# Splitting the first four chunks of an FFN that follows block-sparse attention: half of the units early, the rest behind later chunks

## The chip, the cores and the metric

The kernel runs on one core of a Trainium2 chip. The metric is the device time of one execution in microseconds (us), the median of several runs. The engines are PE (TensorE, matmuls), PEld (its weight loads), DVE (VectorE), ACT (ScalarE), POOL (GpSimd) and SP (SyncE, which here only issues DMAs).

## What is computed

Block-sparse attention over 4 batches, 8 heads, 768 rows and 64 columns per head, in blocks of 32 rows, and then a feed-forward network with a rational function in the middle. A row block sees its neighbours, the first and the last block and three sampled ones; the first and the last block see everything.

```python
mask = np.abs(blk_i - blk_j) <= 1
mask = mask | (blk_i == 0) | (blk_j == 0) | (blk_i == n_blocks - 1) | (blk_j == n_blocks - 1)
...                                                  # and three sampled key blocks per query block
scores = np.where(mask, scores, -1000000000.0)
attn = np.exp(scores - np.max(scores, axis=-1, keepdims=True))
attn = attn / (np.sum(attn, axis=-1, keepdims=True) + 1e-09)
x = (attn @ v)                                       # then heads side by side: 3072 tokens x 512
h = x @ w_in                                         # 512 x 2048
P = a[0] + a[1] * h + a[2] * h * h + a[3] * h * h * h
Q = 1.0 + np.abs(b[0]) * np.abs(h) + np.abs(b[1]) * h * h
out = (P / (Q + 1e-6)) @ w_out                       # 2048 x 512
```

q, k and v are float32; the weights of the FFN arrive as float64.

## The kernel before

**Tiling.** The 3072 tokens are 12 chunks of 256 (three per batch). The 2048 hidden columns are 8 units of 256. One unit of one chunk is 24 matmuls into `ph` (L1078 to L1080, split float16 x against split weights), the rational function on ACT and DVE (L1085 to L1123), and 12 matmuls into the single accumulator `acc` (L1135, L1137, L1141). When a chunk's eight units are through, ACT copies `acc` to a load slot `ld` and SP stores it.

**Attention** goes by pairs of row blocks. `block(j)` gives the row block of position j; a usual pair is one part, the pair of the first and the last block (at position `J`) is three. A part is scores (L834), masked maxima on DVE (L846), exp on ACT (L865), transposes of the probabilities on PE (L914), values (L960) and the division (L986); 14 parts make a batch, 56 all. Batch 0 reads its keys from SBUF ("near", through the tile `kx`); for later batches the turned keys are stored to DRAM (`ks`) and POOL gathers them for each part into a key buffer (L792 to L801): one buffer is the front part of `kall`, which holds batch 0's keys until its last near scores, two more are made when the weights are decoded. Values are gathered by SP (`vg`, L929 to L939). Every four blocks, x is turned and split into float16 halves in one of three buffers: for chunks below `XD` by PE (`turn_x`, L999), for later ones by transposing DMAs (L1025).

**Weights** are decoded from float64 on the chip, in 16 pieces of w_in (two units each take four) and 16 of w_out (two per unit): ACT, POOL or DVE converts, DVE packs the bits (L452, L455, L459) and makes the low parts (L525), POOL subtracts (L475). Each piece has a due place: the first place in `order` at which its unit is wanted.

**Order.** Every operation is an `Op` with an engine, a price, what it follows, and a due time `prio` counted in places of the list `order`. `issue` builds the instruction streams: of the operations that are due no more than 8 places ahead of the last unit issued, it takes the one that can start first by the prices, and by due time among those; the streams are then fixed. `Ring` and `Slot` stand for buffers. `order` lists (chunk, unit); the list index is the place. Before, chunk 0 runs units 0 to 3, chunk 1 all eight, chunk 0 units 4 to 7, and then chunk by chunk. The first half's sum of chunk 0 waits in two of the three load slots (`kept`). `part_prio` gives the due time of attention parts, `when` that of a batch's preparation. PE fills idle time with matmuls of no use (L162) until the first accumulator is in use.

Of the kernel before, what the change touches and what calls it, by code (L numbers as in the profile page):

```python
# [11 lines left out]
F32 = mybir.dt.float32  # L12
# [12 lines left out]
def kernel(  # L25
# [27 lines left out]
    nc = tc.nc  # L53
# [230 lines left out]
    r_ld, r_kt = Ring([p3] * 3), Ring([p1])  # L284
    r_ldq, r_qt, r_fc, r_ks = Ring([None]), Ring([None] * 2), Ring([None] * 2), Ring([None] * 2)
    r_xn, r_x16 = Ring([None]), Ring([])
# [56 lines left out]
    def scales(get, name, after, prio, slot=(), finish=None, keep=None):  # L343
# [9 lines left out]
        def largest():  # L353
            m = p4.tile([P, 12], F32, name=name, bufs=3)
            res.append(m)
            nc.vector.tensor_reduce(out=m[:, 0:1], in_=d["pt"][:, :P], axis=AX.X, op=ALU.max)
# [47 lines left out]
    HU = 4  # L404
    order = [(0, u) for u in range(HU)] + [(1, u) for u in range(NU)] + [(0, u) for u in range(HU, NU)] + [(c, u) for c in range(2, NC) for u in range(NU)]
    place = {cu: n for n, cu in enumerate(order)}

    def weights():
# [5 lines left out]
        for u in range(NG):  # L414
            pieces += [(min(place[0, 2 * u], place[1, 2 * u]) + -4.91, 0, u, x) for x in range(NCC)]
        for x in range(NF):
            pieces.append((min(place[0, x // 2], place[1, x // 2]) + x % 2 / 2 + 0.45, 1, x // NCC, x))
        pieces.sort(key=lambda p: p[0])
# [119 lines left out]

    J = (NT // 2 + 1) * TB - 2

# [22 lines left out]
    k_turned = {}  # L563
    ext = []

# [3 lines left out]
    def new_ld(slot):  # L569
        return slot.buf.tile([P, 512], F32, name="ld", bufs=3 if ext and slot.buf is ext[0] else None)  # L570

# [161 lines left out]
    ends = {}  # L733
    kxs = early.tile([P, 2, 2 * NR + 2, HG, BLK], F32, name="kx", bufs=1)

# [6 lines left out]
    def attention(b, j, prio):  # L742
# [296 lines left out]
    last_near = []  # L1039
    XB, XD = 4, 2  # L1040
    x_group = {}


    fcs, o_fc, accs, s_acc, kept = {}, {}, {}, {}, {}

    def factors(b, u, n, after, prio):

        def run():
            if b not in fcs:
                fcs[b] = p2.tile([P, 4, NU], F32, name="fc")  # L1050
# [10 lines left out]
    def unit(c, u):  # L1061

        b, k0 = c // NCH, place[c, u]
        new, last = u == 0 or (c == 0 and u == HU), u == NU - 1 or (c == 0 and u == HU - 1)
        d = {}
        s_ph, s_sq, s_tt, s_ab, s_rr, s_gh, s_gl = [Slot(r) for r in (r_ph, r_sq, r_tt, r_ab, r_rr, r_gh, r_gl)]

        def into(e):
            def run():
                xh, xl = xs_of[c]  # L1070
                d["cst"] = fcs[b][:, :, u]
# [70 lines left out]

        deps = (o_ready[c] + [o_fc[b, u]] if u == 0 else [o_fc[b, u]]) + (in_ready[u * CH // WC] if c < 2 else [])
        pk = [k0 + x for x in FO]
        i0 = Op(TE, 1307, into(0), deps, pk[0], behind=chain.get("into"), takes=[s_ph], uses=[s_xs[c]], unit=k0)
        i1 = chain["into"] = Op(TE, 1307, into(1), [i0], pk[1], uses=[s_ph, s_xs[c]])
        a = Op(SC, 571, square, [i1], pk[2], takes=[s_sq], uses=[s_ph])
# [11 lines left out]
        if new:  # L1159
            s_acc[c] = Slot(r_acc)  # L1160
        wo = out_ready[2 * u] + out_ready[2 * u + 1] if c < 2 else []
        o = Op(TE, 1690, out_high, [h] + wo, pk[11], behind=chain.get("out"), takes=[s_acc[c]] if new else [], uses=[s_gh] + ([] if new else [s_acc[c]]))
# [3 lines left out]
        for t in range(CH // P):  # L1166
            def store(t):
                if u == NU - 1 and (c, t) in kept:
                    s_ob, e, o1 = kept[c, t]
                else:  # L1170
                    s_ob, e, o1 = kept[c, t] = Slot(r_ld), {}, None
                acc = s_acc[c]

                def copy(eng):
# [11 lines left out]

                if o1:
                    a = Op(VE, 602, add, [o, o1], pk[12], uses=[s_ob, acc])
# [6 lines left out]
                if o1:  # L1195
                    s_ob.left -= 1
                Op(SY, [(475, 262144 // len(runs(c % NCH * 2 + t)))] * len(runs(c % NCH * 2 + t)), write, [a], pk[12], uses=[s_ob])
# [42 lines left out]
    for c, u in order:  # L1240
        b = c // NCH
        if b == 0 and u % (WC // CH) == 0 and (b, u) not in o_fc:
            factors(0, u, WC // CH, [scale_ready[u * CH // WC], v_scale[0], o_setup], place[c, u] - 1)
        elif b and (b, u) not in o_fc:
            factors(b, 0, NU, [scale_ready[g] for g in range(NG)] + [v_scale[b]], place[c, u] - 2)
        unit(c, u)

    def switch():
        early_cm.__exit__(None, None, None)
        ext.append(ctx.enter_context(tc.tile_pool(name="ext", bufs=1)))  # L1250
        t = max(o.end for o in decoded + last_near)
        r_ld.free += [(t, ext[0])] * 3
        r_x16.free.append((t, None))
        r_kt.free.append((t, kall[:, NP:NP + KB]))
        for j in range(2):
            kgs.append(ext[0].tile([P, NP, HG, BLK], F32, name=f"xkg{j}"))
            r_kg.free.append((t, len(kgs) - 1))

    Op(None, 0, switch, decoded + last_near, -1)
    ctx.enter_context(tc.manual_schedule(engines={getattr(mybir.EngineType, n) for n in (TE, SC, VE, PO, SY)}))  # L1260
# [30 lines left out]
```

## Time and profile before

| | us |
|---|---|
| median of 3 runs | 812.71 (812.38 to 813.65) |
| the profiled execution | 816.15 |
| its span, first to last instruction | 814.5 |
| PE busy | 769.2 |
| DVE busy | 667.9 |
| ACT busy | 570.8 |
| POOL busy | 228.0 |

A busy PE is pipelined matmuls whose ends are modelled, so it shows that PE is never waited for, not that it runs at its peak. PEclk is the granted share of TensorE's 2.4 GHz. L12 is line 12 of the kernel.

### The profile page before, as it was taken

What the parts mean: (1) busy time and instruction counts of PE and PEld (TensorE: products, weight loads), DVE (VectorE), ACT (ScalarE), POOL (GpSimd) and SP (SyncE); (2) the same over time, 40 slices, a digit from 0 to 9 for tenths busy, and PEclk for the clock granted to TensorE, in tenths of its full rate; (3) what the DMA queues carried; (4) which work ended last, traced back from release to release, by engine and by line L of the source; (5) the groups of instructions that cost most, each with busy time, mean ns of one, the idle gap of its engine ahead of it and who ended that gap; (6) DMA issues with size and microseconds to landing.
All of it is one profiled execution on the core that took longest, in us unless ns stands there. A gap on an engine that the chain in (4) does not pass through costs nothing.

```text
span 814.5 us, 26163 instructions
## 1 busy us (share of the span) xinstructions
PE 769.2 (94%) x10147; PEld 542.9 (67%) x10147; DVE 667.9 (82%) x1567; ACT 570.8 (70%) x1266; POOL 228.0 (28%) x401
## 2 busy tenths in 40 slices
PE   7898867799799998999999999999999999999997
PEld 4556645666577677677776667676776767767774
DVE  3878999999968995888887884887878876889986
ACT  2667875977767769768576769677676758767663
POOL 3506342334731025105332043205422044000000
PEclk9999988999899999999999999999999999999999
DMA  8987966446666866846665974857756746320000
GB/s 218 224 223 237 262 196 218 123 126 183 181 163 174 197 168 182 227 121 195 163 139 153 233 154 151 211 150 195 173 113 157 163 121 197 88 80 14 1 27 27
DMA packets 189916, 128.82 MB, mean 158 GB/s; under 512 B 84672, under 2 KB 170816, under 8 KB 189792
## 3 DMA queue, kind: packets, MB, share of 16 engines
q1 hardware_dynamic: 176640, 91.87, 44.0%
q0 software_dynamic: 13152, 35.28, 15.1%
q8 instruction: 81, 1.33, 0.7%
q14 instruction: 43, 0.35, 0.2%
HBM read 110.83 MB, written 11.01 MB: 150 GB/s over the span
## 4 chain that ended last, share of the span: by engine, by line
PE 79%; DVE 11%; ACT 3%; SPq 2%; issue 2%; DMA 2%; ACTq 0%; DVEq 0%
PE acc L1135 10%; PE ph L1078 10%; PE acc L1141 9%; PE acc L1137 9%; PE ph L1079 9%; PE ph L1080 9%; PE m L834 6%; PE av L960 6%; PE m L914 6%; PE acc L162 2%; PE m L560 2%; DVE tt L1092 1%; DMA ldq<-in_q_dram 1%; DVE pr L846 1%; DVE ab L1116 1%
## 5 line engine op out<-in xcount | busy, mean ns | idle before, releaser
L1078 PE MATMUL ph<-xh,wi 128*128 128x256 f16 x768 | 212.1, 276 | 11.3 <-DVE tt L1095 11.3
L1079 PE MATMUL ph<-xl,wi 128*128 128x256 f16 x768 | 211.7, 276 | 0.0
L1080 PE MATMUL ph<-xh,wi 128*128 128x256 f16 x768 | 211.4, 275 | 0.0
L1085 ACT ACTIVATE sq<-ph,fc 128x512 f32<-128x512 f32 x96 | 65.8, 685 | 104.7 <-PE ph L1080 104.2
L865 ACT ACTIVATE pr<-pr,st 128x256 f32<-128x256 f32 x224 | 110.9, 502 | 11.7 <-DVE st L877 11.5
L1135 PE MATMUL acc<-wo_h,gh 128*128 128x512 f32 x384 | 115.0, 422 | 1.4 <-ACT ld L150 0.7
L1141 PE MATMUL acc<-wo_b,gl 128*128 128x512 bf16 x384 | 99.6, 382 | 1.9 <-DVE gl L1123 1.9
L1137 PE MATMUL acc<-wo_l,gh 128*128 128x512 bf16 x384 | 100.1, 383 | 0.0
L1102 DVE SCALAR_TENSOR_TENSOR ab<-sq,absb,ab 128x512 f32<-128x512 f32 x96 | 73.3, 764 | 30.8 <-ACT ab L1099 30.7
L1113 DVE SCALAR_TENSOR_TENSOR gh<-tt,par,rr 128x512 fp32r<-128x512 f32 x96 | 72.9, 759 | 31.1 <-PE acc L1137 23.7
L1078 PEld LDWEIGHTS <-wi 128*128 128x128 f16 x768 | 76.3, 99 | 32.8 <-DVE tt L1095 9.6
L846 DVE CUSTOM_DVE_ANT_1 pr<-m,bias 128x256 f32<-128x256 f32 x204 | 76.4, 419 | 16.2 <-PE m L834 15.7
L1079 PEld LDWEIGHTS <-wi 128*128 128x128 f16 x768 | 75.9, 99 | 15.5 <-issue 2.9
L150 ACT ACTIVATE pT<-m 128x512 f32<-128x512 f32 x112 | 64.8, 594 | 29.5 <-PE m L914 27.7
L801 POOL DMA_DIRECT2D xkg<-ks x126 | 67.9, 539 | 52.1 <-issue 49.3
L1080 PEld LDWEIGHTS <-wi 128*128 128x128 f16 x768 | 76.0, 99 | 9.5
L914 PE MATMUL m<-ident,pr 128*128 128x128 f32 x448 | 71.5, 290 | 7.4 <-ACT pT L150 5.9
L1106 ACT ACTIVATE rr<-ab 128x512 f32<-128x512 f32 x96 | 60.4, 630 | 25.8 <-DVE ab L1102 23.6
L1092 DVE TENSOR_TENSOR tt<-tt,sq 128x512 f32<-128x512 f32 x96 | 70.7, 737 | 9.2 <-ACT tt L1089 9.0
L1135 PEld LDWEIGHTS acc<-wo_h,gh 128*128 128x128 f32 x384 | 66.5, 191 | 16.5 <-issue 2.2
L1089 ACT ACTIVATE tt<-ph,par,fc 128x512 f32<-128x512 f32 x96 | 75.1, 782 | 0.2
L914 PEld LDWEIGHTS m<-ident,pr 128*128 128x128 f32 x448 | 64.0, 206 | 15.0 <-ACT pT L150 6.3
(151 smaller groups left out, 1335.7 us busy)
## 6 DMA issues: line engine op xcount, KB each, us to landing
vg<-in_v_dram SPq DMA_DIRECT2D x312, 64.0 KB, 3.2
vg<-in_v_dram SPq DMA_DIRECT2D x88, 192.0 KB, 3.7
wl<-in_moe_w_out_dram SPq DMA_DIRECT2D x16, 512.0 KB, 4.3
xkg<-ks POOLq DMA_DIRECT2D x126, 64.0 KB, 3.1
vg<-in_v_dram SPq DMA_DIRECT2D x12, 512.0 KB, 4.5
xkg<-ks POOLq DMA_DIRECT2D x21, 256.0 KB, 3.6
ldq<-in_q_dram SPq DMA_DIRECT2D x20, 256.0 KB, 4.4
out_dram<-ld SPq DMA_DIRECT2D x20, 256.0 KB, 3.2
```

Source lines behind the costliest of these rows:

```text
L846: nc.vector.tensor_tensor_reduce(out=prs[x][:, e, g].rearrange("p (s r) -> p s r", r=BLK), in0=h["sp"][g][:, e], in1=add.rearrange("p (s o ...
L865: nc.scalar.activation(out=prs[x][:, e, g], in_=prs[x][:, e, g], func=AF.Exp, scale=SCALE, bias=st[:, 12 + y:13 + y], accum_out=st[:, 16 + ...
L914: nc.tensor.transpose(pp[:, jj * P:(jj + 1) * P], pr[:, e, g, kt:NS * BLK:2], ident)
L1078: nc.tensor.matmul(o, wh, xh[:, :, cc], start=(cc == 0), stop=False)
L1079: nc.tensor.matmul(o, wh, xl[:, :, cc], start=False, stop=False)
L1080: nc.tensor.matmul(o, wl, xh[:, :, cc], start=False, stop=(cc == NCC - 1))
L1089: nc.scalar.activation(out=d["tt"], in_=d["ph"], func=AF.Identity, scale=d["cst"][:, 3:4], bias=par[:, 2:3])
L1092: nc.vector.tensor_tensor(out=d["tt"], in0=d["tt"], in1=d["sq"], op=ALU.mult)
L1102: nc.vector.scalar_tensor_tensor(out=d["ab"], in0=d["sq"], scalar=absb[:, 1:2], in1=d["ab"], op0=ALU.mult, op1=ALU.add)
L1135: nc.tensor.matmul(acc, g, wo_h[:, f], start=(new and e == 0), stop=False)
L1137: nc.tensor.matmul(acc, g, wo_l[:, f], start=False, stop=False)
L1141: nc.tensor.matmul(acc, g, wo_b[:, f], start=False, stop=(last and e == 1))
```

## The change

Four chunks are split instead of one. Chunks 0 to 3 run units 0 to 3 at places 0 to 15, chunk 4 runs whole at places 16 to 23, and then each second half is followed by a whole later chunk: (0, 4 to 7), (5, all), (1, 4 to 7), (6, all), up to chunk 8; chunks 9 to 11 follow whole. The due places of the weights follow from that: units 4 to 7 are first wanted at places 20 to 23. The split x of chunks 0 to 3 is written to DRAM behind their first unit and read back ahead of unit 4; the partial sums go to DRAM too and are read back, and DVE adds them. The pair of the first and the last block moves to the last position of each batch (chunks 2, 5, 8, 11 instead of 1, 4, 7, 10). x is turned by PE for chunks below 6 instead of below 2. The `kx` tile is kept for the whole kernel and becomes a key buffer when the last near scores are done; behind the decoding come one more key buffer and two load slots instead of two and three. Due times of parts and preparation are moved to fit. The core of the diff:

```diff
-    order = [(0, u) for u in range(HU)] + [(1, u) for u in range(NU)] + [(0, u) for u in range(HU, NU)] + [(c, u) for c in range(2, NC) for u in range(NU)]
+    SPLIT = 4
+    order = [(c, u) for c in range(SPLIT) for u in range(HU)] + [(SPLIT, u) for u in range(NU)]
+    for c in range(SPLIT):
+        order += [(c, u) for u in range(HU, NU)] + [(SPLIT + 1 + c, u) for u in range(NU)]
+    order += [(c, u) for c in range(2 * SPLIT + 1, NC) for u in range(NU)]
     place = {cu: n for n, cu in enumerate(order)}
+    soonest = [min(place[c, u] for c in range(NC)) for u in range(NU)]
...
-            pieces += [(min(place[0, 2 * u], place[1, 2 * u]) + -4.91, 0, u, x) for x in range(NCC)]
+            pieces += [(soonest[2 * u] + -4.91, 0, u, x) for x in range(NCC)]
...
-    J = (NT // 2 + 1) * TB - 2
+    J = NB - 2
...
-    kxs = early.tile([P, 2, 2 * NR + 2, HG, BLK], F32, name="kx", bufs=1)
+    kxs = const.tile([P, 2, 2 * NR + 2, HG, BLK], F32, name="kx")
...
-                early_x = x < 5
+                early_x = x < 4
...
-    XB, XD = 4, 2
+    XB, XD = 4, 6
...
+        split = c < SPLIT
+        new, last = u == 0 or (split and u == HU), u == NU - 1 or (split and u == HU - 1)
+        xk = (c, 1) if split and u >= HU else c
...
+        if split and u == 0:
+            def put():
+                xd_of[c] = scr.tile([P, 2, CB * NCC * BLK], F16, name="xd", bufs=SPLIT)
+                for y in range(2):
+                    nc.sync.dma_start(out=xd_of[c][:, y], in_=xs_of[c][y].rearrange("p b c r -> p (b c r)"))
+
+            o_xd[c] = Op(SY, [(475, 262144)] * 2, put, o_ready[c], k0 + 1.2, uses=[s_xs[c]])
+        if split and u == HU:
+            s_xs[xk] = Slot(r_xs)
+
+            def get():
+                xs_of[xk] = xbufs[s_xs[xk].buf]
+                for y in range(2):
+                    nc.sync.dma_start(out=xs_of[xk][y].rearrange("p b c r -> p (b c r)"), in_=xd_of[c][:, y])
+
+            deps.append(Op(SY, [(475, 262144)] * 2, get, [o_xd[c]], k0 + 5.5, takes=[s_xs[xk]]))
...
+                if split and u == NU - 1:
+                    f = Op(SY, [(475, 262144)], fetch, [o_pd[c, t]], pk[12], takes=[s_ob])
+                    a = Op(VE, 602, add, [o, f], pk[12], uses=[s_ob, acc])
...
                 if u < NU - 1:
-                    s_ob.left += 1
-                    kept[c, t] = s_ob, e, a
+                    o_pd[c, t] = Op(SY, [(475, 262144)], put, [a], pk[12], uses=[s_ob])
                     return
...
-        if c == 2:
-            since = 9.1
         if c == 1:
             return by + (0.56 * (x + 1 - need[1])) - 1
+        if c <= SPLIT:
+            return since + (by - since) * (x + 1 - need[c - 1]) / (need[c] - need[c - 1]) - c
...
-        A = [8.9, 8.52] if b == 1 else [11.69, 8.81]
-        return lambda w, stage, j: p0 - A[stage] + (w * 6 + j) * (([0.5, 0.5] if b == 1 else [0.85, 0.83])[stage])
+        A = [6.5, 5.5] if b == 1 else [11.69, 8.81]
+        return lambda w, stage, j: p0 - A[stage] + (w * 6 + j) * (([0.45, 0.4] if b == 1 else [0.85, 0.83])[stage])
...
+    def switch_keys():
+        t = max(o.end for o in last_near)
+        kgs.append(kxs.rearrange("p y s h r -> p (y s) h r")[:, 0:NP])
+        r_kg.free.append((t, len(kgs) - 1))
+        r_kt.free.append((t, kall[:, NP:NP + KB]))
...
+        kgs.append(ext[0].tile([P, NP, HG, BLK], F32, name="xkg"))
+        r_kg.free.append((t, len(kgs) - 1))
+
+    Op(None, 0, switch_keys, last_near, -1)
+    Op(None, 0, switch, decoded, -1)
```

## Rows read from the trace of the kernel before

**Rows 1.** The page: busy us by engine; busy tenths in 40 slices of the span.

```profile
PE 769.2 (94%) x10147; PEld 542.9 (67%) x10147; DVE 667.9 (82%) x1567; ACT 570.8 (70%) x1266; POOL 228.0 (28%) x401
...
PE   7898867799799998999999999999999999999997
...
DVE  3878999999968995888887884887878876889986
```

**Rows 2.** Windows: stretch and length; PE, PEld, DVE, ACT, POOL busy us; clock, DMA share, GB/s.

```profile
62.00:222.00 160.00, 131.70 (x1875) 95.11 (x1875) 152.96 (x332) 121.89 (x273) 70.98 (x94) 0.91 0.65 191
222.00:304.00 82.00, 82.00 (x1107) 57.95 (x1100) 68.82 (x173) 55.60 (x127) 19.23 (x36) 1.00 0.71 177
304.00:740.00 436.00, 431.69 (x5683) 308.39 (x5682) 344.91 (x825) 317.44 (x714) 118.22 (x211) 1.00 0.62 158
...
755.00:800.00 45.00, 45.00 (x311) 32.04 (x308) 40.19 (x61) 29.33 (x48) 0.00 (x0) 1.00 0.04 13
```

**Rows 3.** Chain of waits, 755 to 800 us: start us, length us, what.

```profile
757.00 0.94 PE acc L1135 x4
...
799.40 0.94 PE acc L1135 x4
```

**Rows 4.** Windows of line L1078 alone: PE and PEld busy, instruction counts in brackets.

```profile
62.00:222.00 160.00, 35.02 (x120) 12.61 (x120) 0.91 0.65 191
222.00:304.00 82.00, 24.33 (x89) 8.77 (x90) 1.00 0.71 177
304.00:740.00 436.00, 126.66 (x464) 45.60 (x464) 1.00 0.62 158
```

**Rows 5.** Windows of line L865 alone: ACT busy, count; clock, DMA share, GB/s.

```profile
0.00:62.00 62.00, 8.80 (x35) 0.94 0.86 220
62.00:222.00 160.00, 22.73 (x87) 0.91 0.65 191
222.00:304.00 82.00, 12.51 (x48) 1.00 0.71 177
304.00:740.00 436.00, 72.74 (x280) 1.00 0.62 158
```

**Rows 6.** Chain of waits, 56 to 135 us.

```profile
121.36 3.03 DVE wi L525 x4
...
128.82 0.33 PE ph L1078
```

**Rows 7.** Waits of PE, 62 to 222 us: total us, times, longest us.

```profile
PE ph L1078 <- DVE tt L1095: 10.6, 5, 4.1
```

**Rows 8.** Chain of waits, 56 to 62 us: one group of transposes of x.

```profile
57.08 0.43 PE m L999 x4
```

**Rows 9.** Groups by line, DVE, whole span: busy us, mean ns, then idle before.

```profile
L1179 DVE TENSOR_TENSOR ld<-ld,acc 128x512 f32<-128x512 f32 x2 | 1.3, 684 | 0.9 <-PE acc L1141 0.9
```

**Rows 10.** The page, DMA issues: count, KB each, us to landing.

```profile
xkg<-ks POOLq DMA_DIRECT2D x126, 64.0 KB, 3.1
```

**Rows 11.** Timeline of PE around 184 and 199 us: start us, length us.

```profile
183.81 0.43 PE L834 MATMUL m<-kall,qt 64*32 64x96 f32 x15
...
198.56 1.10 PE L960 MATMUL av<-vg,pT 128*32 128x64 f32 x64
199.59 1.09 PE L834 MATMUL m<-kall,qt 64*32 64x256 f32 x32
```

**Rows 12.** Timeline of POOL, 190 to 260 us: one gather, first and last issue.

```profile
201.09 0.70 POOL L794 DMA_DIRECT2D kall<-ks  x1 [7.18 <-PE m L834]
...
205.31 0.54 POOL L801 DMA_DIRECT2D kall<-ks  x1 [0.16 <-issue]
```

**Rows 13.** Groups by line and form, DVE and POOL, 62 to 222 us.

```profile
L1092 DVE TENSOR_TENSOR tt<-tt,sq 128x512 f32<-128x512 f32 x15 | 15.1, 1008 | 0.4 <-ACT tt L1089 0.4
...
L475 POOL TENSOR_TENSOR wo_l<-dw,wo_h 128x512 bf16<-128x512 f32 x16 | 23.1, 1450 | 13.5 <-ACT wo_h L150 13.0
```

**Rows 14.** The same for DVE, 304 to 740 us.

```profile
L1092 DVE TENSOR_TENSOR tt<-tt,sq 128x512 f32<-128x512 f32 x58 | 39.8, 686 | 6.3 <-ACT tt L1089 6.1
```

More of the change, by code (lines that the diff above doesn't have):

```diff
@@ L353, in largest @@
         def largest():
-            m = p4.tile([P, 12], F32, name=name, bufs=3)
+            m = p4.tile([P, 12], F32, name=name, bufs=B)
             res.append(m)
@@ L414, in weights @@
         for u in range(NG):
-            pieces += [(min(place[0, 2 * u], place[1, 2 * u]) + -4.91, 0, u, x) for x in range(NCC)]
+            pieces += [(soonest[2 * u] + -4.91, 0, u, x) for x in range(NCC)]
         for x in range(NF):
-            pieces.append((min(place[0, x // 2], place[1, x // 2]) + x % 2 / 2 + 0.45, 1, x // NCC, x))
+            pieces.append((soonest[x // 2] + x % 2 / 2 + 0.45, 1, x // NCC, x))
         pieces.sort(key=lambda p: p[0])
@@ L563 @@
     k_turned = {}
-    ext = []
+    ext, EL = [], 2
     def new_pr():
@@ L569, in new_ld @@
     def new_ld(slot):
-        return slot.buf.tile([P, 512], F32, name="ld", bufs=3 if ext and slot.buf is ext[0] else None)
+        return slot.buf.tile([P, 512], F32, name="ld", bufs=EL if ext and slot.buf is ext[0] else None)
     def keys(b, t, prio, before, slot, new):
@@ L1049, in run @@
             if b not in fcs:
-                fcs[b] = p2.tile([P, 4, NU], F32, name="fc")
+                fcs[b] = p2.tile([P, 4, NU], F32, name="fc", bufs=B)
             nc.vector.scalar_tensor_tensor(out=fcs[b][:, :, u:u + n], in0=coefs.rearrange("p (j o) -> p j o", o=1).broadcast_to([P, 4, n]), scalar=v_inv[b],
@@ L1141, in out_low @@
                 nc.tensor.matmul(acc, g, wo_b[:, f], start=False, stop=(last and e == 1))
-        deps = (o_ready[c] + [o_fc[b, u]] if u == 0 else [o_fc[b, u]]) + (in_ready[u * CH // WC] if c < 2 else [])
+        deps = (o_ready[c] if u == 0 else []) + [o_fc[b, u]] + (in_ready[u * CH // WC] if c <= SPLIT else [])
         pk = [k0 + x for x in FO]
-        i0 = Op(TE, 1307, into(0), deps, pk[0], behind=chain.get("into"), takes=[s_ph], uses=[s_xs[c]], unit=k0)
-        i1 = chain["into"] = Op(TE, 1307, into(1), [i0], pk[1], uses=[s_ph, s_xs[c]])
+        if split and u == 0:
[11 more added lines that the diff above has]
+            deps.append(Op(SY, [(475, 262144)] * 2, get, [o_xd[c]], k0 + 5.5, takes=[s_xs[xk]]))
+        i0 = Op(TE, 1307, into(0), deps, pk[0], behind=chain.get("into"), takes=[s_ph], uses=[s_xs[xk]], unit=k0)
+        i1 = chain["into"] = Op(TE, 1307, into(1), [i0], pk[1], uses=[s_ph, s_xs[xk]])
         a = Op(SC, 571, square, [i1], pk[2], takes=[s_sq], uses=[s_ph])
@@ L1167, in store, with fetch, put @@
             def store(t):
[L1168 to L1171, printed above, removed]
+                s_ob, e = Slot(r_ld), {}
                 acc = s_acc[c]
+                def fetch():
+                    e["ob"] = new_ld(s_ob)
+                    nc.sync.dma_start(out=e["ob"], in_=pd_of[c][:, t])
+                def put():
+                    if c not in pd_of:
+                        pd_of[c] = scr.tile([P, CH // P, DM], F32, name="pd", bufs=SPLIT)
+                    nc.sync.dma_start(out=pd_of[c][:, t], in_=e["ob"])
                 def copy(eng):
@@ L1241 @@
         b = c // NCH
-        if b == 0 and u % (WC // CH) == 0 and (b, u) not in o_fc:
-            factors(0, u, WC // CH, [scale_ready[u * CH // WC], v_scale[0], o_setup], place[c, u] - 1)
-        elif b and (b, u) not in o_fc:
+        if b < 2 and u % (WC // CH) == 0 and (b, u) not in o_fc:
+            factors(b, u, WC // CH, [scale_ready[u * CH // WC], v_scale[b], o_setup], place[c, u] - 1)
+        elif b > 1 and (b, u) not in o_fc:
             factors(b, 0, NU, [scale_ready[g] for g in range(NG)] + [v_scale[b]], place[c, u] - 2)
         unit(c, u)
+    def switch_keys():
[3 more added lines that the diff above has]
+        r_kt.free.append((t, kall[:, NP:NP + KB]))
     def switch():
@@ L1250, in switch @@
         ext.append(ctx.enter_context(tc.tile_pool(name="ext", bufs=1)))
-        t = max(o.end for o in decoded + last_near)
-        r_ld.free += [(t, ext[0])] * 3
+        t = max(o.end for o in decoded)
+        r_ld.free += [(t, ext[0])] * EL
         r_x16.free.append((t, None))
[L1254 to L1259, printed above, removed]
+        kgs.append(ext[0].tile([P, NP, HG, BLK], F32, name="xkg"))
+        r_kg.free.append((t, len(kgs) - 1))
+    Op(None, 0, switch_keys, last_near, -1)
+    Op(None, 0, switch, decoded, -1)
     ctx.enter_context(tc.manual_schedule(engines={getattr(mybir.EngineType, n) for n in (TE, SC, VE, PO, SY)}))
```

13 lines of the change are left out of this document (4 added, 9 removed).

## The prediction

> **What bounds the kernel now.** The page comes first: PE is busy 94% of the span and DVE 82%, yet the slices say that these averages hide two stages: up to the eleventh slice DVE is the fuller engine, behind it PE is at 9 throughout [rows 1]. The windows give the border [rows 2]. From 62 us (first FFN unit) to 222 us DVE is busy 152.96 of 160 us and PE 131.70; from 222 to 304 PE is busy all 82 us and DVE 68.82; from 304 to 740 PE is busy 431.69 of 436 us. So behind 222 only PE work counts, and what can be won lies between 62 and 222. The chain of waits there runs through DVE and through the decoding of the weights on it: the low parts of the input weights at 121.4 us stand ahead of PE's unit at place 4 (chunk 1, unit 0), which starts at 128.8 [rows 6]. PE's longest wait in the window, 10.6 us in all, is for DVE's polynomial [rows 7].
>
> How much does PE lose? I price a unit and an attention part (one pass over scores, exp and values; 56 in all). In the pure FFN stage a unit takes PE 5.30 us (757.00 to 799.40 is eight) [rows 3] and DVE 40.19/45 x 5.30 = 4.73 us [rows 2]. Counts come from 8 matmuls of L1078 per unit and 8 records of L865 per part [rows 4, 5]. From 304 to 740 lie 464/8 = 58 units and 280/8 = 35 parts, so a part, with its share of all preparation, costs PE (431.69 - 58 x 5.30)/35 = 3.55 us and DVE (344.91 - 58 x 4.73)/35 = 2.02 us [rows 2, 4, 5]. From 62 to 222 lie 15 units and 10.9 parts: PE needs 118.2 us of the 160 and loses **41.8**. DVE needs 93.0 for them; the other 60 us of its 152.96 are the decoding (lines L452, L455, L459 and L525) and small preparation. From 222 to 304 (11.1 units, 6 parts) PE needs 80.1 of 82 and loses 1.9. The loss to 304 is 43.7 us.
>
> **The change, part by part.** (1) *Order.* Before, all weights are wanted by place 11, after by place 23; before, chunks 0 to 2 are attended by place 16, after chunks 0 to 4. So DVE's 60 us of decoding lie beside more work in which PE needs more than DVE: 0.57 us more per unit, 1.53 more per part. By place 24 the new kernel has run 24 units and 26 parts (22 of chunks 0 to 4, some 4 of chunk 5), of which 35/8 = 4.4 parts lie ahead of 62 us as now [rows 5]. From 62 us on DVE needs 24 x 4.73 + 21.6 x 2.02 + 60 = 217.1 us, PE 24 x 5.30 + 21.6 x 3.55 = 203.9 us. DVE is still the bound, but by 13 us where it was 35. Were DVE as full as from 62 to 222 (95.6%), place 24 would come at 62 + 227 = 289 us with a loss of 23.2; at 87.7% full nothing is won. I take 92%: between the two, as PE is now itself loaded to 86% there, so that each will at times wait for the other. Then 236 us, place 24 at 298, loss 32.1, **11.6 us won**.
>
> (2) *Turned x of chunks 2 to 5 on PE instead of by DMA.* Eight groups of four transposes at 0.43 us [rows 8] are 3.4 us; the six of chunks 2 to 4 run in PE time that DVE leaves idle (0; without that cover 2.6), the two of chunk 5 cost **0.9**. The conversions on ACT and DVE are replaced one for one.
>
> (3) *Partial sums and x through DRAM.* ACT makes 24 copies before and after. DVE adds eight times instead of twice, six more at 0.684 us [rows 9] = 4.1 us, all behind place 24, where DVE is busy 344.91 of 436 us: 0. There is one accumulator, so the next unit's output waits for two adds in a row, four times; the hand-overs behind the first halves stand at places 3, 7, 11 and 15, in the time that DVE bounds. From below 0 (the next unit's input matmuls cover them), from above 4 x 1.4 = 5.5; I take **1**. The new DMAs are 256 KB each. The reads of x may be issued from two units (10 us) ahead of the unit that wants them; on SP the value loads of the next parts queue behind a write that waits for its copy, and those are issued 0.7 of a unit ahead. The trace shows PE without a wait for such loads behind 304 us, so 0; if each of the 8 writes of a partial sum held them up by one add's time, it is 8 x 0.7 = 5.5 us, most of it in the time that DVE bounds.
>
> (4) *End pairs last, key buffers, slots.* The pair with three parts moves from chunk 1 to chunk 2 of each batch: place 4 then needs eight parts where it now needs ten. The split's partial sums no longer hold two of the three load slots from place 3 on, so batch 1's keys load sooner. The near keys' tile becomes a key buffer right behind the last near scores, where before the second one waited for the decoding. All this is what lets chunks 3 and 4 come in time; I cost it at 0, and the last rival is the price if it fails.
>
> Sum: 11.6 - 0.9 - 1.0 = 9.7. The profiled execution took 816.15 us (span 814.5), 3.4 over the median: 806.4, and for the median **803**.
>
> **A rule against the row.** In the window 62 to 222 DVE's product of two tiles in SBUF took 1008 ns, from 304 on 686; POOL's subtraction for the decoded weights, whose own mean is 1450 ns, runs only in the first [rows 13, 14]. If every unit that meets decoding pays these 0.32 us, nine more units pay 2.9 us. The Trainium skill (SBUF — State Buffer, Who interferes with whom) says that a VectorE instruction with two SBUF inputs and a GpSimd instruction that reads SBUF lock each other out, the second waiting for the whole of the first. By that rule the loss goes by POOL's instructions, whose number doesn't change, and the sum above would stand; the longer rows agree with the lock, but not yet with either count.
>
> **Rivals.** *DVE stays full* (95.6% or better): loss 23.2, so 20.5 won and 1.9 paid: **794**. For it: with PE at 100%, DVE was 89% full from 755 on [rows 2]. Against: no stretch shows both above 95%.
>
> *Dearer units under decoding*, as above: 2.9/0.92 = 3.2 us back: **806**.
>
> *DMA becomes the bound.* The engines' share was 0.65 of 160 and 0.71 of 82 us [rows 2], 162 us of full work; 4.7 parts more at 0.62 x 436/35 = 7.7 make 36, and 8 half-megabyte tiles to DRAM at 191/0.65 = 294 GB/s make 14: 212 us. At the 0.86 of the first 62 us [rows 5] that takes 246.5, loss 42.6: about 1 us won, 1.9 paid: **813**. For it: the value and key gathers are small packets. Against: a part's 7.7 holds the loads of whole batches, of which the stretch needs fewer.
>
> *Batch 1 comes too late (slower).* Chunk 3 must now be attended by place 12. Its gathers overwrite the keys of batch 0, so they start behind the last near scores: now 183.8, and batch 1's first scores come at 199.6, 15.8 us later; the values of the last near part follow its scores by 14.8 us (198.6) [rows 11]. A gather holds POOL 4.8 us (201.1 to 205.9) [rows 12] and lands 3.1 later [rows 10], some 8 us a part: chunk 3 is ready 15.8 + 3 x 8 + 14.8 = 55 us behind the last near scores, chunk 2 about 15 behind them. The four units between them last 39 us at 9.8 us a unit (236/24) and 21 at PE's pace. So there is no stall at the forecast's pace (54 against 55), and up to 19 us if the units run at PE's: it decides from the moment that DVE has no decoding left to fill the wait. Paid once in full: 803 + 19 = **822**. For it: chunks 2 to 4 get four units' time each, where chunk 1 now gets four and each later one eight. Against: two key buffers then, one before, and POOL decoding in between.
>
> **How the numbers follow.** Forecast 0.46 (803), DVE stays full 0.09 (794), dearer units 0.07 (806), DMA 0.13 (813), batch 1 late 0.25 (up to 822, of which half beyond 819). Range 793 to 819: below lies half of the full case, above half of the late one. Faster by over 0.2% (1.6 us, about what a measurement of this kernel can tell from no change): 0.46 + 0.09 + 0.07 = 0.62; within: 0.13; slower: 0.25.
>
> **What would show it.** In the new trace: place 24 at about 298 us with about 26 parts done; DVE at 92% between 62 and there, and decoding spread to about place 22; PE without gaps behind it, with the gain to that place not given back. Wrong: PE idle around places 12 and 16 for gathered keys or values (late batch 1); DMA above 0.85 with PE waiting for vg (DMA); PE waiting for partial sums or for x read back, which I cost at 1 us; the 1008 ns row spread over 24 units.

## The result

The changed kernel takes **820.68 us** (median of 5 runs, 817.45 to 824.89) against 812.71 before (5 runs, 811.77 to 813.65). The ratio is 1.010, 95% interval 1.0078 to 1.0123: slower by 1%, where 803 us and a range of 793 to 819 were forecast. The profiled execution took 821.29 us, its span 819.6.

The page of the changed kernel: busy us by engine, and the tenths in 40 slices, as [rows 1].

```profile
PE 763.0 (93%) x10098; PEld 542.8 (66%) x10174; DVE 671.7 (82%) x1581; ACT 574.8 (70%) x1268; POOL 218.4 (27%) x374
...
PE   7887789989898789899999999899999999999997
...
DVE  3867989679779979998888886677888888877985
```

The windows of [rows 2], columns as there:

```profile
62.00:222.00 160.00, 141.58 (x2541) 105.24 (x2554) 129.32 (x363) 124.25 (x308) 74.05 (x121) 0.97 0.83 223
222.00:304.00 82.00, 73.46 (x1005) 52.51 (x1012) 72.20 (x176) 68.09 (x154) 25.73 (x33) 0.96 0.82 246
304.00:740.00 436.00, 421.60 (x5074) 301.09 (x5119) 366.84 (x805) 303.13 (x648) 97.40 (x162) 1.00 0.54 137
```

Up to 222 us PE is busier than before (141.58 against 131.70) and DVE less (129.32 against 152.96), as was meant. From 222 to 304 us, where PE was busy all 82 us, it now lacks 8.5 us: the gain was there, and was given back. Behind 304 it seems to lack 14.4 of 436 us (before 4.3). Most of that is not idle time: the changed kernel's trace has 45 matmul records fewer than weight loads there (5074 and 5119; before 5683 and 5682), and at some 0.22 us each (four output matmuls take 0.88 us) they make an estimated 10 us.

The loss by the prediction's prices (time since 62 us, less 5.30 us for each unit ahead of the place and 3.55 us for each part done by then, but for the 4.4 parts that the kernel before had done by 62 us; the start of the unit at a place gives the time) shows where. Each row is one profiled execution, and the executions stand up to 3.4 us from the medians of their kernels, so differences of 2 or 3 us between rows mean little. "Slot kept" and "no second decoding" (the second half of the weights is not decoded) are experiments, told below.

| PE's loss up to place, us | 8 | 16 | 24 | 28 | 48 | 60 | span |
|---|---|---|---|---|---|---|---|
| before | 28 | 47 | 40 | 41 | 46 | 49 | 814.5 |
| changed | 19 | 25 | 46 | 49 | 48 | 58 | 819.6 |
| before, slot kept | 24 | 41 | 34 | 35 | 37 | 41 | 803.4 |
| changed, slot kept (batches 2 and 3) | 19 | 23 | 39 | 42 | 46 | 51 | 812.9 |
| before, slot kept, no second decoding | 19 | 13 | 15 | 13 | 15 | 18 | 781.2 |
| changed, slot kept, no second decoding | 17 | 19 | 26 | 24 | 24 | 28 | 790.1 |

At place 16 the changed kernel is 22 us ahead; at place 24 it is 6 us behind. The border between its two stages is place 16, at 242 us (before at 238); place 28 comes at 347 us (before 321). The windows of these two stages, first of the changed kernel, then of the one before:

```profile
62.00:242.00 180.00, 161.18 (x2808) 119.58 (x2826) 145.00 (x404) 140.21 (x345) 77.82 (x128) 0.97 0.83 224
242.00:347.00 105.00, 90.08 (x1039) 61.58 (x1045) 98.53 (x207) 81.51 (x173) 44.11 (x49) 0.95 0.70 211
```

```profile
62.00:238.00 176.00, 147.70 (x2049) 105.51 (x2050) 165.88 (x368) 130.81 (x297) 80.34 (x111) 0.92 0.65 191
238.00:321.00 83.00, 80.93 (x1148) 59.61 (x1146) 64.81 (x160) 60.95 (x141) 20.47 (x37) 1.00 0.71 180
```

The roles have changed places. Before, DVE is the full engine of the first stage (165.88 of 176, 94%) and PE of the second. Now PE carries the first (DVE 81%) and DVE the second (98.53 of 105, 94%). The decoding is what moved: in the changed kernel's second stage DVE packs the last units' weights.

```profile
L530 DVE SCALAR_TENSOR_TENSOR wi<-wo_l,scw,wi 128x512 f16<-128x512 f32 x3 | 2.2, 743 | 0.0
...
L460 DVE SCALAR_TENSOR_TENSOR dw<-wl,dw 128x512 int32<-128x512 int32 x8 | 5.9, 733 | 0.0
L464 DVE SCALAR_TENSOR_TENSOR dw<-wl,dw 128x512 int32<-128x512 int32 x8 | 5.4, 680 | 0.0
L457 DVE TENSOR_SCALAR dw<-dw 128x512 int32<-128x512 int32 x8 | 3.8, 479 | 3.7 <-POOL dw L154 3.7
```

(DVE's groups by line and form, changed kernel, 242 to 347 us: `dw` is w_out, `wi` the last two units' w_in.) Before, no packing is left behind 206 us.

### The profile page after: what moved, and what is told of

The parts are those of the page before. It is cut to its first block, busy times and chain, and to the rows that moved or that the text cites. A ratio compares the mean times of both kernels' runs of the same rounds, so it can differ in the third digit from the quotient of the medians.

```text
span 819.6 us, 26125 instructions
## 1 busy us (share of the span) xinstructions
PE 763.0 (93%) x10098; PEld 542.8 (66%) x10174; DVE 671.7 (82%) x1581; ACT 574.8 (70%) x1268; POOL 218.4 (27%) x374
## 4 chain that ended last, share of the span: by engine, by line
PE 72%; DVE 7%; issue 5%; DMA 5%; SPq 5%; ACT 3%; POOL 2%; POOLq 0%; ACTq 0%; DVEq 0%
PE acc L1142 9%; PE ph L1085 9%; PE acc L1148 9%; PE ph L1086 8%; PE ph L1087 8%; PE acc L1144 8%; PE av L965 5%; PE m L919 5%; PE m L839 5%; DMA vg<-in_v_dram 3%; PE acc L162 2%; SPq L944 2%; SPq L722 2%; PE m L565 1%; DMA ldq<-in_q_dram 1%
## 5 line engine op out<-in xcount | busy, mean ns | idle before, releaser
L870 ACT ACTIVATE pr<-pr,st 128x256 f32<-128x256 f32 x224 | 111.3, 503 | 14.4 <-DVE st L882 14.2
L1148 PE MATMUL acc<-wo_b,gl 128*128 128x512 bf16 x365 | 96.1, 383 | 4.5 <-DVE gl L1130 2.1
L1144 PE MATMUL acc<-wo_l,gh 128*128 128x512 bf16 x327 | 88.8, 384 | 3.9
L1109 DVE SCALAR_TENSOR_TENSOR ab<-sq,absb,ab 128x512 f32<-128x512 f32 x96 | 73.6, 767 | 22.4 <-ACT ab L1106 22.2
L1120 DVE SCALAR_TENSOR_TENSOR gh<-tt,par,rr 128x512 fp32r<-128x512 f32 x96 | 72.3, 754 | 22.3 <-ACT rr L1116 12.5
L1099 DVE TENSOR_TENSOR tt<-tt,sq 128x512 f32<-128x512 f32 x96 | 67.4, 702 | 8.9 <-ACT tt L1096 8.9
L1126 DVE SCALAR_TENSOR_TENSOR tt<-tt,par,ab 128x512 f32<-128x512 f32 x96 | 73.2, 763 | 0.6
L965 PE MATMUL av<-vg,pT 128*32 128x64 f32 x3584 | 63.9, 221 | 8.9 <-DMA vg<-in_v_dram 7.5
```

The costliest lines, as they stand in the source:

```text
L870: nc.scalar.activation(out=prs[x][:, e, g], in_=prs[x][:, e, g], func=AF.Exp, scale=SCALE, bias=st[:, 12 + y:13 + y], accum_out=st[:, 16 + ...
L965: nc.tensor.matmul(d["av"][rows, e, g], pT[:, 2 * g + kt, rows], vf[:, head(h4, g), kt * D:(kt + 1) * D], start=(kt == 0 and (n == 1 or (m ...
L1109: nc.vector.scalar_tensor_tensor(out=d["ab"], in0=d["sq"], scalar=absb[:, 1:2], in1=d["ab"], op0=ALU.mult, op1=ALU.add)
L1144: nc.tensor.matmul(acc, g, wo_l[:, f], start=False, stop=False)
L1148: nc.tensor.matmul(acc, g, wo_b[:, f], start=False, stop=(last and e == 1))
```

## The experiments

Times are medians, ratios stand to the kernel before as run beside them.

**1. How many chunks to split.** The edit is the one constant.

```diff
-    SPLIT = 4
+    SPLIT = 1      # split1; split2: 2; split3: 3
```

> The changed kernel with one split chunk instead of four, which is the order of before (chunk 0 in halves around chunk 1); the end pairs last, the x turned on PE up to chunk 5, the key buffer made of kx, the due times and the way through DRAM of chunk 0 stay. Theory A and theory B alike: the order alone costs the time, so this comes back to 811 to 816. If one of the other edits costs it (end pairs last, key buffers, transposes on PE), it stays at 818 or more.

> The changed kernel with two split chunks: chunks 0 and 1 in halves, chunk 2 whole at places 8 to 15, the weights of units 4 to 7 first wanted at place 12 instead of 20. Theory A: the second half is decoded from some 120 us on, beside attention, DVE is full earlier and never idles for 36 us, so place 24 comes by 305 and the time is 805 to 813. Theory B: less is asked of DMA at once than with four chunks, in between before and after: 813 to 818.

> The changed kernel with three split chunks: the weights of units 4 to 7 first wanted at place 16. Theory A: the decoding piles up less than with four and more than with two, where it no longer does, and the attention ahead of it fills PE better than with two: 808 to 816, between the 810.0 of two and the 820.7 of four. If four chunks are slow for a reason that has a threshold (a buffer or a slot that three chunks still leave free), it is at 811 or less.

One split chunk: 815.6 us (1.0044, 1.0021 to 1.0066). Two: 810.0 (0.9973, 0.9951 to 0.9995). Three: 820.0 (1.0084, 1.0051 to 1.0117). So the time doesn't rise evenly with the split (no run shows why), and the other parts of the change cost 0.4%, some 3 us, with one split chunk alone. Two split chunks win a quarter of a per cent; experiment 5 shows what that is worth.

**2. Weights earlier, partial sums later.** `early8` makes the second half's weights due eight places earlier; `late` fetches the partial sums just ahead of the add; `late_e4` does the second and makes the weights due four places earlier.

```diff
-    soonest = [min(place[c, u] for c in range(NC)) for u in range(NU)]
+    soonest = [min(place[c, u] for c in range(NC)) - (8 if u >= HU else 0) for u in range(NU)]
...
-                    f = Op(SY, [(475, 262144)], fetch, [o_pd[c, t]], pk[12], takes=[s_ob])
+                    f = Op(SY, [(475, 262144)], fetch, [o_pd[c, t]], k0 + 7.5, takes=[s_ob])
```

> The changed kernel, with the weights of units 4 to 7 due 8 places earlier (loads and decoding alike); nothing else. Theory A (the decoding of the second half comes too late: DVE idles 36 us of 62 to 260 us and is then full from 260 to 340): DVE fills that idle time, its busy time from 62 to 222 rises from 129 to at least 145 us, place 24 comes before 300 us instead of at 319, and the time falls by 12 to 20 us, to 801 to 809. Theory B (DMA is the bound from 140 to 300 us, share 0.82 to 1.0, so the weights cannot land sooner, or displace the gathers of the values): the loads are issued sooner but PE waits for vg instead, place 24 stays at 310 to 325, time 816 to 825.

> The changed kernel with the reading back of a partial sum due 5 places later (7.5 places behind unit 4 of its chunk instead of 2.6), so that it holds its load slot for some 3 units instead of up to 10. Theory H (hand-over): from 498 to 519 us PE's output matmuls stood still because ACT's copy of the accumulator waited for a load slot, two of the five being held by sums read back at 471 and 490 us and three by batch 3's keys; with the slots free the output of place 48 starts within 12 us of that of place 47 instead of 26, the loss between places 48 and 60 falls from 10 us to 3, and the time falls by 5 to 9 us, to 812 to 816. If the end pairs or batch 3's preparation stall PE there for themselves, it stays within 3 us of the changed kernel.

> As the kernel with the later read-back, and the weights of units 4 to 7 due 4 places earlier. Theory A and H together: the decoding is spread between 200 and 300 us instead of 254 to 328, DVE is full for less of the time behind place 16, the loss at place 28 falls from 49 to 42 us or less, and with the free hand-over the time is 806 to 811. If earlier decoding only moves the loss ahead of place 16 (as 8 places earlier did: 38 us at place 16 instead of 25, 42 at place 28), it is 810 to 815.

`early8`: 824.3 us (1.013, 1.0068 to 1.0192). It loses 38 us by place 16 and 42 by place 28, where the changed kernel has lost 25 and 49: decoded early, the weights cost PE nearly as much as decoded late. (Between places 48 and 60 it loses 25 more, with PE waiting 4.3 us for batch 3's gathered keys.) `late`: 816.9 (1.0053, 1.0025 to 1.008), 4 us better at most; the slots that it frees at place 47 went to key and value loads. `late_e4`: 831.5 (1.0214, 1.0175 to 1.0253), 54 us lost by place 20.

**3. The way through DRAM, and part of the packing.** `nodram` has no transfers and adds for the split; `nodec` leaves out two of DVE's packing steps for the second half of w_out.

```diff
             def pack2():
+                if kind and x >= NF // 2:
+                    return
...                                       # nodec: the same in pack3
```

> The changed kernel without the way through DRAM: the split x is neither written nor read back (the second halves multiply what lies in the buffer), the partial sums are not written, read or added (of chunks 0 to 3 only the second half's sum is stored). 32 DMAs of 256 KB and 8 adds less. Theory A: these DMAs wait for nothing that sets the end, so the time stays within 4 us of the changed kernel, 817 to 823, with decoding as late as now. Theory B: 8 to 14 us of full DMA work are gone ahead of place 24, the weights come sooner, and the time falls to 806 to 813.

> The changed kernel with the same order of instructions on every engine, less two of DVE's three packing instructions for each of the 8 pieces of the output weights of units 4 to 7 (16 instructions of 0.7 us, 11.6 us of DVE; their weights are wrong). Theory A: DVE is full from 281 to 328 us with these pieces and PE waits for it, so nearly all of it comes off the time: 8 to 12 us less, 809 to 813, and place 28 comes some 10 us earlier. If instead the loads of these pieces (issued from 250 on) bound that stretch, DVE only waits longer and the time stays within 3 us.

`nodram`: 818.0 us (1.0064, 1.0047 to 1.0082), so the transfers, x read back and the adds cost some 2.7 us by the medians; the interval overlaps that of the changed kernel (1.0078 to 1.0123), so it may be nothing. `nodec`: 816.3 (1.0047, 1.0016 to 1.0078), 4.4 us for 11.3 us less DVE work (the 5.9 and 5.4 us of L460 and L464 above). Neither is the 18 us that separate forecast and result.

**4. The hand-over of the accumulator.** In the changed kernel 28 us pass from the first output matmul of unit 15 to that of unit 16, and 26 us from unit 47 to 48, where a unit takes PE 5.3 us; between the last output matmul of one unit and the first of the next they stand still for 25 and 22 us. In the second of these gaps, ACT's copies of `acc` come 7.4 us apart (timeline of ACT; of SP; of PE, 488 to 522 us):

```profile
511.14 0.60 ACT L150 ACTIVATE ld<-acc 128x512 f32<-128x512 f32 x1
...
518.55 0.60 ACT L150 ACTIVATE ld<-acc 128x512 f32<-128x512 f32 x1 [2.21 <-DMA out_dram<-ld]
```

```profile
489.68 0.35 SPq L1196 DMA_DIRECT2D ld<-pd  x1
501.91 0.56 SPq L591 DMA_DIRECT2D ld<-in_k_dram  x1
509.08 0.36 SPq L657 DMA_DIRECT2D ld<-in_v_dram  x1
510.70 0.37 SPq L591 DMA_DIRECT2D ld<-in_k_dram  x1
514.11 0.52 SPq L1213 DMA_DIRECT2D out_dram<-ld  x1
```

```profile
492.96 1.17 PE L1142 MATMUL acc<-wo_h,gh 128*128 128x512 f32 x4
...
496.19 0.81 PE L1148 MATMUL acc<-wo_b,gl 128*128 128x512 bf16 x3 [0.16 <-issue]
...
519.20 1.21 PE L1142 MATMUL acc<-wo_h,gh 128*128 128x512 f32 x4 [1.58 <-ACT ld L150]
```

The second copy waits until the first one's slot is stored: the other slots hold a fetched partial sum and batch 3's keys and values. So I let those loads start only while two slots are free; one is then always left for the copy.

```diff
         o_ld = Op(SY, [(475, 262144)], load, () if first else [sc_of[2]], prio - 1, takes=[slot], behind=before)
+        if b >= 1:                        # 2 in b_res and res_b2
+            o_ld.rings[r_ld] = 2
...                                       # the same for the loads of the values
```

> The changed kernel, with one rule more for its planner: a load of keys or values of batches 1 to 3 may take a load slot only while two are free, so that one slot is always left for the copy of the accumulator (and for the partial sums that come back). Theory, hand-over starved of slots: in the changed kernel the output matmuls stood still for 28 us between units 15 and 16 and for 26 us between units 47 and 48 because the copies of the accumulator waited for slots that key and value loads held. With the slot kept back both gaps fall to 14 us or less, the loss of TensorE at place 24 falls from 46 to some 36 us, and the time falls from 820.7 to 806 to 814 us. Rival, VectorE full: the loss between places 16 and 28 comes from the packing of the second-half weights that runs with VectorE at 20.0 of 20 us from 260 to 340 us; then the gaps may shrink, but the loss at place 24 stays at 44 us or more and the time stays within 4 us of 820.7. Second rival, keys late: the loads that are held back make batch 1's scores late, the loss at place 8 rises from 19 to 25 us or more, and the time is 823 us or more.

> As the run before, and the partial sums are fetched back just ahead of the end of a second half (due 7.5 places after its start instead of with the last unit's due time of the planner's list), so that they hold a load slot for less time. Theory, starved slots: both gaps at 14 us or less, and 2 to 4 us less than the run before in the second one, 804 to 812 us. Rival, VectorE full: no more than the late fetch alone gave (816.9 us), within 4 us of it.

> Two chunks split instead of four, with one load slot kept back from keys and values. Two split chunks alone gave 810.0 us; its only long gap of the output matmuls at a hand-over is 19 us between units 47 and 48. Theory, starved slots: that gap falls to 14 us or less and the time by 3 to 6 us, to 804 to 807 us. Rival, VectorE full: 808 to 812 us, since nothing changes before place 24.

`res`: 815.0 us (1.0008, 0.9987 to 1.003), 5.7 better. The gaps (from first to first) fell from 28 to 19 and from 26 to 14 us, but the loss at place 24 stayed at 45: the slots are a cost, and not that of places 16 to 24. `res_late`: 818.4 (1.0051, 1.0027 to 1.0075), a miss; the later fetch doesn't add to it. `s2_res`: 808.1 (0.9939, 0.9911 to 0.9966); with the late fetch it was 810.9 (0.9961).

**5. The same slot in the kernel before.** The edit is the one above, for batches 2 and 3.

> The kernel before, with one load slot kept back from the keys and values of batches 2 and 3. Here the output matmuls stand still for 24 us between units 23 and 24 and for 22 us between units 47 and 48. Theory, hand-over starved of slots (a cost that both kernels have): both gaps fall to 15 us or less and the time by 3 to 7 us, to 806 to 810 us, so that half of the gain of two split chunks with a slot kept back (808.1 us) is not the split's. Rival, slots scarce only with the split: gaps within 3 us of 24 and 22, time within 2 us of 813.

> The changed kernel, with one load slot kept back from the keys and values of batches 2 and 3 alone, the same rule as in the kernel before with a slot kept back (806.85 us). Theory, the slots and the change are two costs that add up: 814 to 817 us, some 8 us more than the kernel before with the same rule, as without the rule (820.7 against 812.7). Rival, the rule for batch 1 was what cost it: 806 to 810 us.

`b_res`: **806.85 us** (0.9931, 0.9911 to 0.995), the fastest kernel here that does all of the work. Its gaps of 24 and 22 us (from first to first), between units 23 and 24 and 47 and 48, fell to 9 each. `res_b2`: 815.71 (1.0046, 1.0023 to 1.0069). So the starved hand-over was in the kernel before too, it costs 5 to 6 us in either, and it explains nothing of the difference: 8.0 us without the rule, 8.9 with it. And two split chunks with the rule are no better than none with it.

**6. What the put-off decoding costs.** `res_nodec3` takes `res` and leaves out 18 us of DVE's packing; `res_early4` makes it due four places earlier.

```diff
             def pack2():
+                if x >= NF // 2 if kind else u == NG - 1:
+                    return
...                                       # the same in pack3, and for w_in in pack1
```

> The changed kernel with one load slot kept back from keys and values (815.0 us, TensorE's loss 19 us at place 16 and 45 us at place 24), from which VectorE's packing of the last two units' w_in and of the second half of w_out is left out (12 instructions of 0.41 and 0.68 us and 16 of 0.68 us, 18.0 us together; the weights of the second halves' units are therefore wrong in value). The other engines' steps, the loads and the order of the instructions stay. Theory, VectorE full: the 26 us lost between places 16 and 24 are VectorE's packing that was put off, so at least two thirds of the 18 us come back: the loss at place 24 is 27 to 33 us and the time 797 to 804 us. Rival, loads late: the second half's weights arrive too late whatever VectorE does (they are fetched from 241 to 315 us), so the loss at place 24 stays at 40 us or more and the time at 811 us or more.

> The changed kernel with one load slot kept back from keys and values, and the weights of the second halves due four places earlier. Theory, VectorE full: VectorE was idle 25 us in 117:242 of the changed kernel, so packing that is done there is free: loss at place 16 up from 19 to at most 27 us, at place 24 down from 45 to 36 us or less, time 804 to 811 us. Rival, loss conserved: TensorE pays for the packing whenever it is done, as with the weights eight places earlier (38 us at place 16, 45 us at place 24): loss at place 24 within 4 us of 45 and the time 813 to 820 us.

`res_nodec3`: 811.0 us (0.9988, 0.9972 to 1.0003): at most some 4 us for 18 us of DVE work, as its interval overlaps that of `res`. The theory of a full VectorE asked for 797 to 804 us and fell; the loss at place 24 is 38 us (45 in `res`), and that in an execution 4.5 us faster than its median. So DVE's time alone isn't it. The windows of the stage from place 16 to place 28, of `res` and then of `res_nodec3`:

```profile
236.00:344.00 108.00, 91.17 (x1040) 63.41 (x1045) 98.27 (x207) 80.37 (x171) 38.96 (x49) 0.91 0.73 206
```

```profile
233.00:335.00 102.00, 89.25 (x1076) 62.38 (x1065) 82.92 (x180) 80.12 (x173) 39.26 (x51) 0.97 0.78 222
```

DVE is 81% busy and the stage 6 us shorter, no more, and the granted clock differs too (0.97 against 0.91), so that part of the 6 us may be the clock's. What holds PE there: PE's waits from 300 to 311 us, and the timelines of DVE and of ACT.

```profile
PE acc L1156 <- DVE gl L1138: 6.2, 2, 5.7
```

```profile
304.70 0.46 DVE L458 TENSOR_SCALAR dw<-dw 128x512 int32<-128x512 int32 x1 [4.42 <-ACT dw L150]
305.07 0.67 DVE L1131 SCALAR_TENSOR_TENSOR ab<-ab,gh 128x512 f32<-128x512 f32 x1
305.78 0.75 DVE L1134 SCALAR_TENSOR_TENSOR tt<-tt,par,ab 128x512 f32<-128x512 f32 x1
306.57 1.64 DVE L1138 TENSOR_TENSOR gl<-tt,rr 128x512 bf16<-128x512 f32 x1
```

```profile
304.00 0.66 ACT L150 ACTIVATE dw<-wl 128x512 f32<-128x512 f32 x1 [3.63 <-DMA wl<-in_moe_w_out_dram]
```

DVE stands at a packing step whose words were fetched at 298 us; ACT, which converts them, waits for the load until 304. The unit's own steps are queued behind the packing in DVE's order, and PE waits for `gl`. The same wait stands in `res`, with all of the packing (waits of PE and of DVE, 236 to 344 us):

```profile
PE acc L1152 <- DVE gl L1134: 8.7, 2, 7.8
```

```profile
DVE dw L457 <- ACT dw L150: 5.4, 1, 5.4
```

`res_early4`: 815.1 (1.0038, 1.0019 to 1.0057), no gain; it loses 28 us by place 16 (19 without), 56 by place 24 (45) and 47 by place 28 (46).

So the whole decoding of the second half was taken out, loads and all, in both orders.

```diff
-        for u in range(NG):
+        for u in range(NG // 2):
             pieces += [(soonest[2 * u] + -4.91, 0, u, x) for x in range(NCC)]
-        for x in range(NF):
+        for x in range(NF // 2):
...
-                f = 2 * u + e
+                f = (2 * u + e) % (NF // 2)
```

> As the run before, but the second halves of the FFN's units take the weights of the first halves: the loads, the conversions and the packing of the second half (16 loads of 512 KB, and on VectorE 8 times 2.5 us for w_in and 8 times 1.8 us for w_out, 34 us) are left out, and the output is that of other weights. Theory, put-off decoding: what the changed kernel loses between places 16 and 28 (27 us with a slot kept back) is the decoding of the second half, by VectorE's time or by its loads; without it the loss at place 28 is 25 us or less and the time 790 to 798 us. Rival, the order: after place 16 there are only some five parts of attention to stand between the units, so units in a row keep losing at the hand-overs; loss at place 28 of 35 us or more, time 803 us or more.

> The kernel before with one load slot kept back from the keys and values of batches 2 and 3, in which the second halves of the FFN's units take the weights of the first halves: the same loads, conversions and packing are left out as in the run before. Theory, put-off decoding: the decoding costs the same in both orders or less in this one, so without it this kernel comes to 785 to 795 us and both lie within 4 us of each other. Rival, the order: the kernel with the changed order stays 6 us or more behind this one.

| median us (ratio, interval) | order before | changed order | difference |
|---|---|---|---|
| slot kept | 806.85 (0.9931, 0.9911 to 0.995) | 815.71 (1.0046, 1.0023 to 1.0069) | 8.9 |
| and no second decoding | 784.82 (0.9661, 0.9631 to 0.9691) | 790.45 (0.9735, 0.970 to 0.977) | 5.6 |
| the second decoding | 22.0 | 25.3 | |

The decoding of the second half costs 22.0 us in the old order and 25.3 in the new; each ratio is known to 0.2 to 0.35%, up to 3 us, so the two aren't told apart, and no gain from putting it off is to be seen. The loss between places 16 and 28 is the decoding: 19 us in `res_b2`, 5 without. But the changed order is slower by 5.6 us without that decoding, and there the intervals don't touch, if narrowly. The windows of `b_res_alias` and then `res_alias`, 62 to 322 us:

```profile
62.00:322.00 260.00, 243.72 (x3488) 177.73 (x3517) 209.82 (x499) 188.53 (x431) 81.91 (x135) 0.99 0.66 172
```

```profile
62.00:322.00 260.00, 244.93 (x3847) 180.82 (x3869) 204.80 (x533) 195.67 (x467) 97.21 (x165) 0.98 0.78 208
```

PE is as busy in both, and over the spans it is idle 32.7 us (781.2 - 748.5) and 31.6 (790.1 - 758.5). (Some of both is not idle: 82 and 76 matmul records are missing beside the weight loads.) So the new order has no more idle time; PE is busy for longer. Of those 10 us of busy time 4.1 are the turning of x (PE's groups by line, `b_res_alias`, then `res_alias`):

```profile
L1004 PE MATMUL m<-ident,xn 128*128 128x128 f32 x16 | 3.2, 319 | 2.9 <-DVE xn L991 1.6 <-DVE st L851 1.3
```

```profile
L1009 PE MATMUL m<-ident,xn 128*128 128x128 f32 x48 | 7.3, 274 | 0.0
```

Another part belongs to this pair of executions and not to the orders. The granted clock was 0.996 over the span of `b_res_alias` and 0.989 over that of `res_alias`, 3.1 and 8.7 us withheld, so an estimated 5 us at most are the clock's. Over all the runs the clocks were alike (0.989 to 0.997 and 0.988 to 0.997), and the medians stand 5.6 us apart where the spans of this pair stand 8.9. What is left lies in pieces of 1 to 2 us over scores, values and unit matmuls. No run turns x by DMA in the new order, so how much of the 5.6 us the turning makes isn't settled.

## Why the prediction was wrong

**Step (1), the order, failed, in the 92%.** Its demand was right: DVE was forecast to need 217.1 us from 62 us to place 24 and was busy 216.52, with two parts more done than forecast (28 for 26) and some of the packing left behind. But place 24 came at 319 us (forecast 298), DVE 84% full, and PE had lost 46 us there where 32.1 were forecast. I took one fullness for one stretch in which "each will at times wait for the other". The stretch is two stages. Up to place 16 the order puts attention: 15.75 units and 20 parts, 154.5 us of PE's 180, and DVE has little to do, since the later weights aren't due. From there to place 28 it puts 12 units and 5 parts, 81.4 us of PE's work, beside all the decoding left: 105 us. A sum over both, 203.9 for PE and 217.1 for DVE, lets DVE's idle 35 us of the first stage be filled with the packing of the second; nothing in the order does that. The larger of two sums is less than the sum of the larger ones, stage by stage. That is a part of it: to place 28 DVE needs 243.5 us in all, the larger needs of the two stages (154.5 for PE, 98.5 for DVE) make 253.0, and 285 passed. The other 32 us were lost inside the stages, 25.5 in the first and 6.5 in the second. Of those in the first, 15 are lost by place 4, while the first half is decoded; no run here takes that stage apart.

What the forecast took for 11.6 us won was therefore lent: 22 us at place 16, repaid by place 28. Experiment 6 shows what the repayment is: without the second half's decoding 5 us are lost between places 16 and 28 instead of 19. More than DVE's own time goes into it, as a late load stops DVE in its own order (5.4 us in `res`, 4.4 in `res_nodec3`); how much of the whole is of that kind no run measures.

**Step (2), x turned on PE,** was mis-sized. I paid 0.9 of 3.4 us, since PE would be idle anyway while DVE decodes. PE's busy time for it rose by 4.8 us, from 2.9 for 16 transposes on the line before to 7.7 for 48 (forecast 3.4), and from places 4 to 16 the changed kernel loses only 10 us in which they could hide: the change itself took most of the cover away. That the cover failed is argued, not shown. For it: 4.1 us of busy time stand beside the 5.6 us of the order alone, and with one split chunk the other edits together cost 3 us.

**Step (3), DRAM,** was put at 1.0 between 0 and 5.5; `nodram` gives 2.7, not clear of noise. **Step (4)** was put at 0. For the slots that held as a difference (8.0 without the rule, 8.9 with it), but my reason, that the split no longer holds load slots, didn't: the hand-over starved for slots in both kernels, and I had not seen the 24 and 22 us in the trace of before, though the sixteenth slice of PE, in a row that I read as 9 throughout behind the eleventh, is an 8 [rows 1]: the first of these gaps begins in it, at 309 us.

**The rivals.** *DVE stays full* (794): 84%. *Dearer units* (806): the dear rows did spread. From 242 to 347 us DVE's L1126 took 886 ns on average, against 746 from 400 to 700, where POOL subtracts nothing; and twelve of them make 1.7 us. The Trainium skill (SBUF — State Buffer, Who interferes with whom) fits that row; no run here tells it from another cause. But the sum did not grow with the units. Over a unit's six rows with two inputs in SBUF (L1099, L1109, L1120, L1123, L1126 and L1130; mean less that of 400 to 700 us, times the count) it was 10.7 us for 16 units before (62 to 238 us), and 4.8 + 5.7 = 10.5 us for 27 units in the two stages of the changed kernel. So it fits the count of POOL's subtractions (16 before; 14 and two on DVE in the changed kernel), not the one by units, which asked for 2.9 us more. *DMA* (813): the share was 0.83 from 62 to 242 us and PE waited 7.5 us for values in the whole span; the 0.86 that I took for a ceiling is none, as from 180 to 200 us the share was 1.01 with PE busy 19.04 us of 20. Late loads count in another way, through DVE's order. *Batch 1 too late* (822): the number is near, the mechanism isn't there, so the nearness is luck. The loss is 19 us at place 8 against 28 before, and still 19 at place 12 against 36, and PE's longest waits of the changed kernel are short:

```profile
PE av L965 <- DMA vg<-in_v_dram: 7.5, 6, 2.2
PE m L565 <- DMA ldq<-in_q_dram: 5.9, 2, 4.4
PE ph L1085 <- DVE tt L1102: 3.7, 3, 1.6
```

I named "the gain to that place not given back" as a sign, and had the wrong place: 24, when the repayment starts at 16.

## What to carry to other kernels

Work that is put off isn't hidden: before a busy share is forecast for a long stretch, cut the stretch where the order changes its mix, and take the larger engine of each piece; that gives a lower bound (here 253 of 285 us). Count what is queued behind a step that waits for a late load in its engine's order, beside the step's own time. And look for the resource that two streams share in silence, here the load slots (three; behind the decoding six before, five in the changed kernel). One rule that keeps a slot for the accumulator's copy won 0.7% on the kernel before, more than any version of the split without it.

## What was not expected

Packing 18 us less on DVE, in a stage in which DVE is 91% busy (`res`), gave at most some 4 us. In its place DVE waited, as the two windows of experiment 6 show: the full engine was not the bound by itself; in the piece shown, a load that landed late held it as well.
